# A mask DMA put behind q's low half, twelve weight chunks converted on one engine less, and another order of work

## The chip, the cores and the metric

The kernel runs on one core of one Trainium2 chip. The metric is the device time of one execution in microseconds (us). TensorE is called PE below (its weight loads PEld), VectorE DVE, ScalarE ACT, GpSimd POOL, SyncE SP.

## The reference, cut to what matters

```python
# attention: batch 2, 8 heads, 768 positions, head size 64, 16 cluster centres a head
q_assign = argmax(q_n @ c_n);  k_assign = argmax(k_n @ c_n)
scores = where(q_assign[:, None] == k_assign[None, :], q @ k.T / 8, -1e9)
x = softmax(scores) @ v                        # 1536 tokens x 512
h = x @ w_in                                   # 512 -> 2048
g = where(h >= 1, h, where(h <= -1, 0, (h + 1) ** 2 / 4))
x = g @ w_out                                  # 2048 -> 512
out = ((x @ w1) * (x @ w2)) @ w3 @ w_out2      # 512 -> 1024 -> 1024 -> 512
```

All arithmetic is float32. The weights come to the kernel as float64 words.

## The kernel before

**Work and stages.** Matrix products in float32 precision are made of products of a high and a low half (`hi`, `lo`): x = hi + lo, and three of the four partial products are summed. Attention goes by units: unit u is a pair of heads of one batch (u = 0 to 3 batch 0, 4 to 7 batch 1), each with heads h = 0 and 1. A unit has two groups of 384 query positions and in each of them six tiles s of 128 queries against 768 keys, so 48 tiles a batch (`s` 0 to 47 and 48 to 95). A tile is `s` (PE, scores), `smax` (DVE, L867), `sbias` (POOL, L872), `sexp` (ACT, L880), `spT` (PE, transpose, L897), `sT` (copy to SBUF, ACT or DVE), and six tiles later `pv` (PE, product with v). Batch 0's attention runs beside the preparation of the last two weight matrices (`wp`, L1169: w3 @ w_out2 beforehand); after it come the MLP products of batch 0 beside batch 1's attention, then the MLP of batch 1 alone.

**Halves of q and k.** For head h of a unit, `kh` and `qh` copy the high halves into place, `klo` and `qlo` subtract to get the low halves (POOL or DVE), `k2h`, `q1h` and `qh0` copy a half to the other partitions. Tile kq2 holds q's and k's high halves; its rows 64 to 79 carry, at the time of the product, the cluster mask. For h = 1, `qh` (L678) first writes q's high half into rows 64 to 127 of kq2, `qlo` (L690) reads it there, and `qh0` (L684) puts a copy into rows 0 to 63. The operation `k2` (`kq_fill`, L713) fetches the mask rows by two DMAs on ACT's queue (batch 0), one for each half of the columns. `s` needs `klo`, `qlo`, `k2`, `k2h` and `q1h` of its head.

**Weight chunks.** `chunk` (L1094) loads 128x512 float64 words as pairs of 32-bit words and makes float32 of them: `wl` (DMA on ACT's queue), `wabs` (ACT, L1107: the high word as a float, scaled, so that its bits lie right but for a shift by 3), `wr` (ACT, L1111: the low word scaled by 2^-29, in place, written as an integer), `wc 2` (DVE, L1115: shift left by 3, or the low bits), `wc 3` (DVE, L1121: or the sign). Then `whi` (ACT or DVE) and `wlo` (POOL or DVE) split the chunk, or, for chunks that are kept for later, `wd` writes it to DRAM (SP's queue). Chunks 0 to 39 are converted while batch 0's attention runs, 40 to 71 in the MLP of batch 0.

**The order.** The program's order is written out: ORDER (L38) has two characters for each of 3036 operations; they are a number in base 88 whose half is the operation's place in the sequence of `add` calls, and whose last bit chooses the first or the second engine that the operation may run on. `order` (L126) reads it, and every engine gets its instructions in that order. So a position below is a place in ORDER, and an engine works its own operations off one behind the other. A `needs` entry binds the order to come; the semaphores themselves follow from the order and from what each instruction reads and writes. Forty `idle` operations (L469) are dummy matmuls that stand among the first 60 PE operations.

Of the kernel before, what the change touches and what calls it, by code (L numbers as in the profile page):

```python
# [13 lines left out]
U32 = mybir.dt.uint32  # L14
AF = mybir.ActivationFunctionType
ALU = mybir.AluOpType
# [27 lines left out]
    ",(+m<8<s<6&D<F+w&9%@+y+|,#,*,,,6<:<<&K<J<L<N&I,.+e,8,:,<&N,%<g,0<?<@,2,><V<w<e=*,@,L,B,N,D,F+g,P,R,X,Z,]=:,_"
    "<i<Z;|<0<2<k<]<n,e<p<`<a,T,H,J,V,a+i+l,u,w,y&P<u<y<|=J=#-(&@-*-,+o<B<Q<R=,=.=0,c,|-#=X-4-6=<=>=@,g&B&L=i-.-%"
    "-8=2-:&S+r=y=5=6=B=D+s<q=%=(-0-2=N=L-<-@-B,i-D=P=R&T=U=V->=]>0=Z-F&c=m>@-L-X>#=k,k-N-Z=_=a&Y=o,m,o=d-u-H-P-R"
    "-w=q=s>P=|-]&_,r=f-_-e-g-J-y>%=8=F>2=H>a&k>4-a.(.*.,-T,s-V-c>(&[>o>+>6>8&W>:>D-|=g&e=u=w>-?#&b>B>F%*&^%B>H.4"
    ".#...%.6.8&m&i&v>K>L>T-i-k-m-o?4>e.@.0.B.3>.>=>>>R>V&g.:&s?(-q.L.N>X>Z.<.X.Z>c>g>i>q&o>s>u>N.D.F.P.R.T.H.>?F"
    ">l?%?*>w?,>z>n>~.]._.u.a?V.J.V>]?@-s?.?0.c>_/4/(/*/,&z($/@/B.w?2?B?D&w?i?8.m?6?y(-(&%,/.?H&q&|((%D.y?X.|?J/#"
    "?Z/6/8?:?<?>/:/0/<?L?]?N?_?a/%?k?m?o.e/2.g/>?P/D@2?R?q?s?u%.%0%2%4%F/L/N/P/F@B/H?c/J?|@#%H@T/R%6@4%J@,(.?T?e"  # L50
    "?g/X@e%8%:%<0(%L/Z.i.k.o/T0*@6(*@F/]/_@%@(@*.q.s/V@8@:@=@>?w/a/c@./u/w@0@X@D@i0,0.@w/y/|0406%N/m@V@N@H@J/e/g"
    "@L%P0#00%R%T@Z@g@k@]@mA.@o080:@`0%02@b@@@P@R@y0<0>0@0L0B0D0N0P@|A#0X/i/k/oA@AP@qA:A%A)A*0u0w0y0F@c@s0R0H0T@u"
    "0ZA0A20K0WAcA4/rA6A8A,A<A>0]0_0|ADABAF/s(0(2(4(61#0a0cAsAH0e0g1(1*1,14161&ARAgAJAMATAV1.AeAiAk181:AXA]AZ0m10"
# [1704 lines left out]
```

## Time and profile before

| | us |
|---|---|
| three runs | 718.83, 718.34, 717.74 (median 718.34) |
| the profiled execution, its own time | 718.73 |
| its span, first to last instruction | 717.0 |
| PE busy in the span | 697.8 |
| DVE busy | 617.9 |
| ACT busy | 466.6 |
| POOL busy | 278.0 |

Busy is the time in which an engine had an instruction in work; for PE the ends are modelled. Stretches are given from the span's start. 1.7 us of the profiled execution lie around its span.

### The profile page before, as it was taken

How to read it: one execution, taken by the hardware profiler on the slowest of the kernel's cores; microseconds unless marked ns; L12 is line 12 of the kernel's file. 1: busy time of each engine (PE TensorE's matmuls, PEld its weight loads, DVE VectorE, ACT ScalarE, POOL GpSimd, SP SyncE). 2: the span in 40 equal slices, each digit the busy share in tenths (PEclk: the TensorE clock that was granted, in tenths of full speed). 3: DMA queues.
4: the chain of work that ended last, by engine and by line, in shares of the span. 5: the costliest groups of instructions: out<-in, count | busy, mean ns of one | idle time of the engine just before them, and what ended most of it. 6: DMA issues, size and time to landing. Idle time of an engine off the chain costs nothing.

```text
span 717.0 us, 11999 instructions
## 1 busy us (share of the span) xinstructions
PE 697.8 (97%) x4173; PEld 631.0 (88%) x4173; DVE 617.9 (86%) x1091; ACT 466.6 (65%) x871; POOL 278.0 (39%) x349
## 2 busy tenths in 40 slices
PE   5999999999999999999999999999999999999998
PEld 2866777667798999899999999999999999999997
DVE  6989999989888799988999998669988888999941
ACT  7989999878796976897867565235844434544210
POOL 3333524221354522444363232315842643188500
PEclk9999999999999999999999999999999999999999
DMA  8356786876989988998989996654122121222121
GB/s 316 124 196 216 253 257 199 284 236 212 238 189 187 220 228 198 194 261 216 236 218 234 232 221 161 163 200 135 59 74 75 59 88 30 75 75 59 59 81 67
DMA packets 125645, 122.37 MB, mean 171 GB/s; under 512 B 83792, under 2 KB 92432, under 8 KB 125584
## 3 DMA queue, kind: packets, MB, share of 16 engines
q1 hardware_dynamic: 103024, 62.18, 35.4%
q10 hardware_dynamic: 22560, 59.42, 26.4%
q8 instruction: 33, 0.54, 0.3%
q14 instruction: 28, 0.23, 0.1%
HBM read 75.79 MB, written 22.28 MB: 137 GB/s over the span
## 4 chain that ended last, share of the span: by engine, by line
PE 80%; ACT 7%; DVE 7%; DMA 3%; issue 2%; ACTq 0%; POOL 0%; SPq 0%; DVEq 0%
PE mo L1239 37%; PE sc L1492 8%; PE sc L859 8%; PE sc L1239 6%; PE mo L1492 5%; PE mo L1169 3%; PE av L976 3%; PE av L968 3%; PE av L1492 2%; PE sc L897 2%; DVE nm L867 2%; ACT pt L352 1%; ACT w L1111 1%; PE av L1239 1%; DMA pt<-phl 1%
## 5 line engine op out<-in xcount | busy, mean ns | idle before, releaser
L1239 PE MATMUL mo<-X,whl 128*128 128x384 f32 x924 | 170.4, 338 | 0.0
L1239 PEld LDWEIGHTS mo<-X,whl 128*128 128x128 f32 x924 | 160.7, 188 | 2.8 <-issue 0.9
L1239 PE MATMUL mo<-G,whl 128*128 128x384 f32 x720 | 133.3, 340 | 0.0
L1239 PEld LDWEIGHTS mo<-G,whl 128*128 128x128 f32 x720 | 126.6, 188 | 1.1 <-issue 0.3
L357 POOL TENSOR_TENSOR whl<-wf,whl 128x512 fp32r<-128x512 f32 x61 | 83.0, 1363 | 102.6 <-ACT whl L352 51.8
L867 DVE TENSOR_REDUCE nm<-sc 128x1 f32<-128x768 f32 x96 | 89.9, 950 | 11.2 <-PE sc L859 11.0
L872 POOL TENSOR_SCALAR nm<-nm 128x1 f32<-128x1 f32 x96 | 32.0, 334 | 126.9 <-DVE nm L867 123.3
L352 ACT ACTIVATE whl<-wf 128x512 fp32r<-128x512 f32 x69 | 43.1, 627 | 43.8 <-PE mo L1239 16.1
L859 PE MATMUL sc<-k,q 128*128 128x512 f32 (+1 forms) x192 | 53.7, 361 | 4.2 <-ACT pt L352 2.6
L1111 ACT ACTIVATE w<-w,down 128x512 uint32<-128x512 uint32 x72 | 54.3, 764 | 3.4 <-DVE wf L1121 2.4
L357 DVE TENSOR_TENSOR phl<-sc,phl 128x768 f16<-128x768 f32 x46 | 43.7, 951 | 10.6 <-ACT phl L352 10.1
L1107 ACT ACTIVATE wf<-w 128x512 f32<-128x512 f32 x72 | 48.1, 671 | 5.4 <-DMA wd<-wf 2.1
L1115 DVE SCALAR_TENSOR_TENSOR wf<-wf,w 128x512 uint32<-128x512 uint32 x72 | 49.0, 685 | 1.9 <-ACT wf L1107 1.2
L1121 DVE SCALAR_TENSOR_TENSOR wf<-w,wf 128x512 uint32<-128x512 uint32 x72 | 49.2, 690 | 0.9
L880 ACT ACTIVATE sc<-sc,nm 128x768 f32<-128x768 f32 x46 | 39.8, 866 | 15.2 <-POOL nm L872 15.0
L859 PE MATMUL sc<-kq 80*128 80x512 f32 (+1 forms) x192 | 49.5, 339 | 0.0
L880 ACT ACTIVATE P<-sc,nm 128x768 f32<-128x768 f32 x50 | 44.8, 898 | 7.1 <-POOL nm L872 2.3
L357 DVE TENSOR_TENSOR whl<-wf,whl 128x512 fp32r<-128x512 f32 x51 | 39.7, 779 | 7.3 <-ACT whl L352 7.0
L859 PEld LDWEIGHTS sc<-k,q 128*128 128x128 f32 x192 | 31.5, 189 | 12.7 <-ACT pt L352 5.5
L897 PEld LDWEIGHTS sc<-ident,P 128*128 128x128 f32 x300 | 33.5, 140 | 9.6 <-ACT P L880 5.9
L897 PE MATMUL sc<-ident,P 128*128 128x128 f32 x300 | 39.5, 275 | 2.1 <-ACT P L880 2.0
L1239 PE MATMUL sc<-G,whl 128*128 128x384 f32 x204 | 37.8, 339 | 0.0
(235 smaller groups left out, 1435.1 us busy)
## 6 DMA issues: line engine op xcount, KB each, us to landing
wf<-wd ACTq DMA_DIRECT2D x64, 256.0 KB, 2.8
w<-in_w_out_dram ACTq DMA_DIRECT2D x24, 512.0 KB, 5.1
wd<-wf SPq DMA_DIRECT2D x48, 256.0 KB, 3.5
w<-in_w3T_dram ACTq DMA_DIRECT2D x16, 512.0 KB, 3.9
w<-in_w_in_dram ACTq DMA_DIRECT2D x16, 512.0 KB, 4.7
w<-in_w_dram ACTq DMA_DIRECT2D x16, 512.0 KB, 4.8
wp<-wf SPq DMA_DIRECT2D x16, 256.0 KB, 3.2
wf<-wp ACTq DMA_DIRECT2D x16, 256.0 KB, 2.9
```

The source lines that it names most:

```text
L352: nc.scalar.activation(out=out, in_=in_, func=AF.Copy)
L357: (nc.gpsimd if e == "POOL" else nc.vector).tensor_tensor(out=out, in0=a, in1=b, op=ALU.subtract)
L859: nc.tensor.matmul(ps[:, n], q[0:n_rows, q0:q0 + 128], k[0:n_rows, n], start=first, stop=not first)
L867: nc.vector.tensor_reduce(out=nm, in_=T[("sc", b), s], axis=AX.X, op=ALU.max, negate=True)
L880: nc.scalar.activation(out=new(("P", b), s).rearrange("p n s -> p (n s)") if by_pe(s) else T[("sc", b), s], in_=T[("sc", b), s], func=AF.E ...
L897: nc.tensor.transpose(T[("sc", b), s][:, c], p[:, c], ident)
L1107: nc.scalar.activation(out=T["wf", i], in_=T[w64, i].bitcast(F32)[:, :, 1], func=AF.Abs, scale=float(2.0 ** -112))
L1111: nc.scalar.activation(out=lo, in_=lo, func=AF.Identity, scale=float(2.0 ** -29 - 2.0 ** -41), bias=down)
L1115: nc.vector.scalar_tensor_tensor(out=w, in0=w, scalar=3, in1=T[w64, i][:, :, 0], op0=ALU.logical_shift_left, op1=ALU.bitwise_or)
L1121: nc.vector.scalar_tensor_tensor(out=w, in0=T[w64, i][:, :, 1], scalar=0x80000000, in1=w, op0=ALU.bitwise_and, op1=ALU.bitwise_or)
L1239: nc.tensor.matmul(acc, w[:, a, k4 * 128:(k4 + 1) * 128], rhs(c, k4), start=(first and k4 == 0 and n == 0), stop=(last and k4 == 3 and n = ...
L1492: nc.tensor.matmul(ps, lhs(av, a, k), rhs(bv, c, k), start=k == 0 and n == 0, stop=k == 1 and n == 2,)
```

## The change

Three edits. First, the need of `k2` in batch 0 for h = 1 is `qlo` in place of `qh`. In the old order `k2` stands ahead of `qlo` for units 1 and 2 (positions 220 and 224, 438 and 468), and behind it for units 0 and 3; in the new one it stands behind it for all (25 and 107, 210 and 239, 432 and 447, 567 and 619).

Second, for chunks 1, 3, ... 23, `wr` on ACT is left out. DVE does it: `wc 1` (tensor_scalar, shift left by 3, in place) and `wc 2` (scalar_tensor_tensor, low word shifted right by 29, or the result).

Third, ORDER is another string of the same length. PE's operations of batch 0's attention follow nearly the same sequence. What differs ahead of the last `pv` of batch 0 (position 885 in both), read from the two strings, is where operations run:

| operation | ACT before, after | DVE before, after | POOL before, after |
|---|---|---|---|
| wr | 40, 28 | | |
| wc 1 to 3 | | 80, 92 | |
| klo, qlo | | 12, 7 | 8, 13 |
| kh, qh, qh0, k2h, q1h | 26, 30 | 15, 11 | |
| sT | 42, 41 | 6, 7 | |
| ri (reciprocal rows to SBUF) | 5, 7 | 3, 1 | |
| whi | 6, 8 | 19, 17 | |
| wlo | | 9, 10 | 16, 15 |

`klo` and `qlo` of batch 1 are on POOL 6 times before and 11 times after. At the start `qlo 0 0` and `klo 0 0` go from DVE to POOL; POOL's sequence becomes `qlo 0 0`, `klo 0 1`, `klo 1 0`, `qlo 1 0`, `klo 0 0`, `sbias 0` (before: `klo 0 1`, `klo 1 0`, `qlo 1 0`, `sbias 0`). On ACT `qh 1 0` stands right behind the first mask (`ah 0 k 5 0`); before, a second mask instruction (`am0 k 0`) stood between them. `k2 1 0` goes from position 235 to 86.

```diff
@@ ORDER: all lines
-    "###%#*#,#0#.#(#2$2$V%X%[#4%e%h$.%V%c%q$0$6$8$:#R#>%b$<%m$X$]#D$_$a#8#:%k%_:m$>%y&,:|;0%]%i$c$4$H$J;>#V$@$B$D"
...
+    "###*#,#%#0#(#.#2#4$V%X%Z$.%c$X$0$4$]%e%q%V%i%_%y:m%h%m:|;0;>%];L&,$6$8$:$<$_$a$>$c$e$2$H#P$@$B$J$g$Z$q#H$s$,"
...
@@ k2
-                    else [("qh", u, h)] + [("ah", 0, w, 5, j // 2) for w in "kq"],
+                    else [("qlo" if h else "qh", u, h)] + [("ah", 0, w, 5, j // 2) for w in "kq"],
@@ chunk
+        def shift(e):
+            w = T["wf", i].bitcast(U32)
+            nc.vector.tensor_scalar(out=w, in0=w, scalar1=3, scalar2=None, op0=ALU.logical_shift_left)
+
+        def low(e):
+            w = T["wf", i].bitcast(U32)
+            nc.vector.scalar_tensor_tensor(
+                out=w, in0=T[w64, i][:, :, 0], scalar=29, in1=w, op0=ALU.logical_shift_right, op1=ALU.bitwise_or
+            )
...
-            add(("wr", i), {"ACT": 0.56}, t - 8.5, low_floor, [("wl", i), "c_const"])
-            add(("wc", i, 2), {"DVE": 0.6}, t - 7.8, shift_low, [("wabs", i), ("wr", i)])
+            if i % 2 and i < 24:
+                add(("wc", i, 1), {"DVE": 0.34}, t - 8.2, shift, [("wabs", i)])
+                add(("wc", i, 2), {"DVE": 0.6}, t - 7.8, low, [("wc", i, 1)])
+            else:
+                add(("wr", i), {"ACT": 0.56}, t - 8.5, low_floor, [("wl", i), "c_const"])
+                add(("wc", i, 2), {"DVE": 0.6}, t - 7.8, shift_low, [("wabs", i), ("wr", i)])
```

## Rows read from the trace of the kernel before

**Rows 1.** Windows: PE, PEld, DVE, ACT, POOL busy (count), PEclk, DMA share, GB/s.

```profile
0.00:18.00 18.00, 10.14 (x57) 4.58 (x58) 12.45 (x33) 13.45 (x18) 5.84 (x15) 1.00 0.85 315
18.00:198.00 180.00, 173.56 (x1057) 129.58 (x1056) 167.59 (x266) 157.91 (x273) 58.24 (x85) 1.00 0.70 221
198.00:702.00 504.00, 502.52 (x3000) 485.64 (x2999) 436.30 (x791) 294.76 (x581) 213.04 (x250) 1.00 0.60 150
```

**Rows 2.** Windows within 18 to 198 us, the same columns.

```profile
18.00:72.00 54.00, 51.30 (x334) 39.50 (x333) 49.92 (x84) 49.42 (x86) 18.75 (x28) 1.00 0.54 179
72.00:126.00 54.00, 53.57 (x312) 39.62 (x310) 51.38 (x80) 51.85 (x90) 20.51 (x25) 1.00 0.72 236
126.00:198.00 72.00, 68.69 (x417) 50.45 (x415) 66.29 (x104) 56.63 (x99) 18.97 (x33) 1.00 0.79 241
```

**Rows 3.** Waits, 0 to 198: who, for whom; total us, times, longest.

```profile
PE sc L859 <- ACT pt L352: 2.6, 7, 1.2
ACT sc L880 <- POOL nm L872: 2.6, 2, 1.7
...
ACT wf L1107 <- DMA wd<-wf: 2.1, 1, 2.1
```

**Rows 4.** Groups, 0 to 198 us: count, busy us, mean ns, idle before.

```profile
L352 ACT ACTIVATE pt<-sc 128x768 f32<-128x768 f32 x42 | 32.7, 808 | 4.7 <-PE sc L897 3.8 <-PE sc L859 0.3 <-DVE nm L867 0.2
...
L1111 ACT ACTIVATE w<-w,down 128x512 uint32<-128x512 uint32 x40 | 30.2, 767 | 1.7 <-issue 1.0 <-DVE wf L1121 0.7
L1115 DVE SCALAR_TENSOR_TENSOR wf<-wf,w 128x512 uint32<-128x512 uint32 x40 | 27.1, 685 | 0.7 <-ACT w L1111 0.4 <-ACT wf L1107 0.2
...
L352 ACT ACTIVATE kq<-kq 64x768 fp32r<-64x768 f32 x10 | 8.4, 837 | 0.6 <-DMA kq<-in_qT_dram 0.5
L357 POOL TENSOR_TENSOR k<-kq,k 64x768 fp32r<-64x768 f32 x4 | 8.2, 2047 | 12.1 <-ACT k L352 8.2 <-DVE k L354 3.9
...
L354 DVE COPY pt<-sc 128x768 f32<-128x768 f32 x6 | 5.6, 949 | 0.0
...
L354 DVE CAST kq<-kq 64x768 fp32r<-64x768 f32 x10 | 5.5, 553 | 0.2
...
L357 DVE TENSOR_TENSOR q<-kq,kq 64x768 fp32r<-64x768 f32 x5 | 4.8, 952 | 1.5 <-DMA kq<-mask 0.9 <-ACT kq L352 0.6
...
L354 DVE CAST whl<-wf 128x512 fp32r<-128x512 f32 x11 | 4.6, 420 | 0.2
...
L352 ACT ACTIVATE whl<-wf 128x512 fp32r<-128x512 f32 x7 | 4.3, 629 | 0.0
...
L357 DVE TENSOR_TENSOR whl<-wf,whl 128x512 fp32r<-128x512 f32 x6 | 4.1, 680 | 0.0
...
L352 ACT ACTIVATE rb<-mo 128x384 f32<-128x384 f32 x5 | 2.4, 486 | 0.8 <-PE mo L954 0.7
...
L354 DVE COPY rb<-mo 128x384 f32<-128x384 f32 x3 | 1.6, 549 | 0.0
```

**Rows 5.** Timeline of 5 to 21 us: start, us, what, [idle before <-releaser].

```profile
10.15 0.58 DVE L555 STREAM_TRANSPOSE P<-sc 128x384 f32<-128x384 f32 x1 [1.45 <-PE sc L539]
...
11.35 0.95 DVE L357 TENSOR_TENSOR k<-kq,k 64x768 fp32r<-64x768 f32 x1
...
16.85 0.84 ACT L352 ACTIVATE kq<-kq 64x768 fp32r<-64x768 f32 x1
...
17.77 1.82 POOL L357 TENSOR_TENSOR q<-kq,kq 64x768 fp32r<-64x768 f32 x1 [3.19 <-ACT kq L352]
...
20.19 0.62 PE L859 MATMUL sc<-k,q 128*128 128x512 f32 x2 [0.26 <-DVE kq L590]
```

**Rows 6.** Waits of 198 to 717, columns as in rows 3.

```profile
ACT sc L880 <- POOL nm L872: 12.4, 11, 2.8
```

**Rows 7.** Lines 354, 357, weights only: ns minimum/median/maximum, first and last start.

```profile
L354 DVE CAST whl<-wf x43: 385/419/1207, 51.1 to 692.4; 128x512 fp32r<-128x512 f32 x43
...
L357 POOL TENSOR_TENSOR whl<-wf,whl x61: 1264/1295/2082, 43.7 to 701.6; 128x512 fp32r<-128x512 f32 x61
```

More of the change, by code (lines that the diff above doesn't have):

```diff
@@ L44 @@
[L44 to L53, printed above, removed]
@@ new lines @@
+    "+B;g&>+D*i*k*o;s+<<T+0+2+L+N+P+X+Z+]<(;u&&<*&/&:<6<,&5<.;x;y&D+F+R+>+_;Z;j;k&<%(<c+H*r*s+T+a+u+J+V<s+c+w+y,4"
+    ",(,*,,,6,8<8<:<F<<<H<J<L<N%%+e&F&I<X+m<?+|,#<@,.,:,0,<&K&8,%=*,2,>,@<V,L,B,D+g=:,N,P,X,Z,]&N<e<g<i<Z<k<]<n,F"
+    ",R;|<`<a<0%><2,u<u<p,_,T,H,J+i,a&@,w+k+o<w<y=J,V=X,y,|,c,e,g<|=#<B<Q<R&P-(-*+r=,=>=<-4-#-6=i&B-,-.=.=0=@=2%@"
+    "=B=D=5-%&M-8-:+s<q=%=(-0-2&c=6-<,i-@-B-D=L=]=y=Z=N=P=_=R=U->>0-X,k-F=a=d=e-L-N,m-P-Z-]&j-H&T-u-w-K=k=V&Z&X>@"
+    "&W=m=o>P>#,o=q-R-_-e=8=F=H-g=s&_.(-a.*=|>2,q-T-V>a-c-y&]-|>D&k,s>%>(>o>4>+>6&S>->8>:>B>F&b>H&n=g=u&o=w&e.4.6"
@@ new lines @@
+    ".#.,...%?#>J>L-m>e-i-k-o.@.0?4.B.3&g&s>.>=>>>R>T.L.N>V.8.:.<.X.Z?(>X%B%*-q>N>c>q>g>Z&u.D.F>s.P.R.T.>>i?F?%?*"
+    ">u?,.]._.H.J.a?V.V.u>w>l?/>n>z&q.c?1>~/(/4>]?@&w(,>_&y&|/@?6?H?i?J(%?Z.w-s?8?X/B/*.y.|/D/,?2?B?D.m($%,/6/8/."
+    ".e()/:%D(.?:?<?>?L?]?_?a/#?m/%/0/<?k?o/2/>?y?N?P?R(*?q?s%.%0%2%4%F/L/N/P/F/H.g?u%H%6%J@2@B/J?c?T?e@#@,?|/X/R"
+    "%L?g%8%:%</Z/]/T@T.i.k.o0(0*0,@%@(@*@4?w@.@0/_.q.s/a/V/c@D/u/w/y%N@F@H@J@L@e0.@6/|@8@:0406@<@w@?A.@X/m00@V/e"
+    "/g@i@N%P%R%T080:@g0#0&02@@@Z@]@_@k@q@m0<0>@a@|@P@y@R@oA:0L0@0N0P0X/i/kA@0B0DA2A#/oA%A)A*0u0w@c@s@u0y0ZAP0R0F"
@@ new lines @@
+    "0T0H0KA0A4Ac0|0]0_0W/rAs/sATA,A<A>0e0a0c0gA6A8AD(01((2ABAR1*1,1.Ag141#1618AFAH(4(6AV0mAXAZAwAJAeAiAM101%120i"
+    "0kAuAkAn0oAo1X1ZA]1@1L(:(91N1BB%B,ANA_(<(>AyA|B#Aa1:1]0r1P(B(M1R(A(N1D1F1<1>1_1e1g(D(FAqB(B*1H1T1J1V1a1d(HFL"
+    "BJBi1i1l0s(J2*2,2.20B/1u1w1y22C.B01|(P(R241m1o1r(T1s(V2#2%BL2(BN26(X28B2B4B6BlB82:2<(ZB>B;C0CLB@2F2H2>2A2B2D"
+    "BBBDBmCk2JB]B_2LBbBc2N2PB=2RBFBPC2CNBRFe2T2VCQB|BTC#C%BIC(BVC@2c2e2X2ZCB2]BX2_CE2gBeBg2i2l2m(]BZBoBqBsCFCmCo"
+    "Bu2a2oD0C*CRCTC,CVBx3%3(D>3*3436CICJFPDL3,CX3/3032C4C6BzC8C:CqCsCuDZCwC=Cz383:C|D33<3>3@D#3B3D3F(_D5CZC^D%(a"
@@ new lines @@
+    "D(G#C_C>3P3R3TDACaDODB2y3H3K3LD63NCcCeD*Di3_DD3V3Y3Z3]G((c(e(gDQD-3mD:2qE.EL3a3c3e3gD.2sDFChD93o3q3i(lDHD]D_"
+    "DK3sD<DR3v3w2u2xDk3k(m3yDVE0EkDTDX(o(j(t(u(q3|40424#4>4@444649DeDh2|DmDa4%EO4BFiF04:4<4D4GE2D|EP4HF>CiDcFNFR"
+    "FT4(DoEnEo4L4N4PE#4Z4]4_E%E(Dq3#GLFgFkFVFm4RE@EB4T4VE*EDE,EFDsE4E6(wDu4J4XF2F4(yDxDyFoE8GuE:EI4a4c4eE<E>4*4,"
+    "EK4.4gG%G*G,(|)#)%G.ER4iETEWE_EaEcF@FB4kGy4mEXGPHDEeEqEh5:5<EsGNGRGTF:GV4oEuEw4qEj4s4uF#5>5@F<5C5D5FFXF6F8FZ"
+    "GwE[Ez4w4yE]F%F(F*E~4|5#G|H#HmF]5,5.F_5%FqFs)()*5(5*HF5H5J5LFHFJI,FDFFF-G0G3HHHJ5NFaFcGY5PGZHL5V5R5T5XHoHq),"
@@ new lines @@
+    ").HsHuHwFyF|ID5Z5]I]5eFu5g5i5_H%Fw)4F/5a5c5k)0H(H*G@GBGDI05mI.)2GFGH5oHNG4G6G8G]G_IFHQGJHRG:GaG<Ia5s5u5w5yGc"
+    "IH6(6*6,GfI2I4Gh5|6#G?IJ)8IL545052Iu565q58GiGkHyH|GmI_I6GoGrGtIc)<H8H:H<H>H,H.H06.60Ie6R6THTHVJDI9H2H4666%Ig"
+    "62INJm);)6)>64HaHcIQ6D6F6VHYH@HfHZ6X6Z6]I:I#I%I(IwHgIy6H6JI|J#JHJFJJHj6a6c6e)@6L6N6_JLISI@IBHkI*6g6iJ%6PH^I<"
+    "I>JqIiJ(J*H`6kIXIZ6o6q6sHBIkJoK4JsJuH6)B6>JN6m)D6uKT6w6y6|K6J87#7%K8K:J:KuJ<J>K<IT)F)H)J)LJQ7(7*JwK>IVIq7N7P"
+    "7RKVKXKZIsJSImJAJzJ|K]K_7,Io7.707TL<68KyJCJ,J.J0J2J5J7JTJVLTJXJZJ^J`)N)P7V7X7ZK@JaJcJeKBJgL@JiJkKwL>6:6<7274"
@@ new lines @@
+    "76K#K%K(787:KaKcLBK*K|LDL#Lu7<7>KDKF7]KHKLKNKPL%K,KJL(LVLX7_7a7c7eK.K1KRL+K2KmKo7k7m7oM47g7iLZ)SKqKsLw7qL]Ly"
+    "6@)T7s7u7wMTL,L4L6L8M8KeL.L0L:LHM6LaKgKiL2LKL|7y7|LF)V)X)ZKk8#8%8(M#MmM(7@M:7BMX8.7H80828486MV8*M<LP8,Ld88LL"
+    "LNM+LR8<8>8@M@LmMCL_)]7D8X8Z8]Lo8BN46BM>MZ8J8_Lq)_7G)h8:LeLgMqLiM]MaMcLsLk8EMD8FM,7J)iM%8HMoM.MF8aM0)aN8MsMu"
+    "My8cNL8g8i8kM|8mN6Nm)kM37LMLN:N<Me8u)cN@NBMiMkMIMKNP)m8L8p8qMNNN8w8yNq8|8eM_8sMw)eMQMhMSN>NRNTNYNZ8RN,N.NHN0"
+    "O,N2)oNo9#N#OLNJ)qNDNsNu)s9%9(O0N%N(9*9,NyNG8N8P989:N]N_O.ONO2N~O4NaOPOe9.90O9O;OR9<9>92OT94NeNgO6NV9@9BP,OX"
@@ new lines @@
+    "OZ96N+O(O*ODOF9FO#OgOHPDOiNcOJ9H9c9e9J9LOkNjOmNkNw9gO&OaOdOqOs9N9P9DOV9RO<O>P0P.P2P49iO@9TP8O]O_Pe9k9q9sOuOw"
+    "OC9m9oOoP;P#9V:%9X9uPHPFPJ8TPL9w9y:(:*9|P%:#Q#P@PN9]PPPS:4PTP)Pi9ZPgP+:,:.8VP6PkPmOzPq:0:2Q(Pt:6Q%PB:8Q*Q,::"
+    ":<O~:>:@P<P>P]:PQDPVQ0Q.PoP_:RPX:B:D:F:H:K:LQN:T:VPu:_:Y:Z:NPyPw:]P|QFQIQ2Q4Q<Q>Q6P[QaQJPaQPQkR#Q@Q9Q:PdQS9_"
+    "9aR.:aQCQLQcQfQTQW:c:fQmQo:gS0QZQ^:iR@QiSASCRcR_S2:kQgR%R)QXR1R3RaR]RfS4RhSEQwQzRjQqQtS6S;Q_S$RyRJS]S_SLRqRm"
+    "S8R|RCS=SPQuQ|RERpSSRtS(S&SfShS+SUR,SmSoSiSqToR*SHSuR:R=S?RlR4SyRFRHRMROR7StTqR8SWSaS,SdT(SxT0RuS/SXSlS[T#Rx"
@@ L96 @@
+    "f#gLfXfif&fmf(hehog6fofqgyh+fZgNgJgHg|h.hgh2h0hih#h4h,hHfkfgfsfugVgXh6h8hrgZg_fwg]hsh(gcgfggh<hBgPgahmhDh>i("
+    "i*hLh@gihJhkhNhThPglgmhRhFhVh_hahci2iDhXi,i.i0h|h[h]hui$iNi4i6i8i>iFiQiIiLi:iaicifiJhwhyi<i%ikiniRiZiiigi^i_"
+    "iTiWiXioiAiqitiBiuiwiyi|"
 )
```

64 lines of the change are left out of this document (18 added, 46 removed).

## The prediction

> **What bounds the kernel now.** I read the stretches first, since a share of busy time over the whole span mixes stages. From 198 to 702 us PE is busy 502.52 of 504.00 us [rows 1]: there PE is the bound, and all that a change of order can win visibly is 1.48 us. The first 18 us have PE busy for 10.14 us; most of the rest passes before its first matmuls, while loads land. Between them, from 18 to 198 us, PE is idle for 180.00 - 173.56 = 6.44 us [rows 1], and here the next two engines are nearly full as well: DVE is busy 167.59 us (93%), ACT 157.91 us (88%), POOL only 58.24 us (32%). The granted clock is 1.00 in all these stretches, the higher of its two levels, so no part of the time is owed to it.
>
> The reader should then cut this stage in three [rows 2]. From 72 to 126 us PE (53.57 of 54.00), ACT (51.85) and DVE (51.38) are all full. From 18 to 72 us PE is idle 54.00 - 51.30 = 2.70 us, and from 126 to 198 us 72.00 - 68.69 = 3.31 us. What PE waits for is seen in the waits [rows 3]: ACT's eviction of the transposed scores ended 2.6 us of PE's idle time in 7 pieces; and ACT itself once waited 2.1 us for the landing of a converted chunk's DMA, because `wabs` of a later chunk needs that buffer. So the stage is bound by three engines in a ring, PE to DVE to ACT to PE, with four score banks between them, and not by one of them.
>
> **The change part by part.** The sums go over the operations ahead of batch 0's last `pv`, counted from the table in the section on the change.
>
> ACT loses 12 `wr` of 767 ns, 9.20 us [rows 4]. It gains 4 copies of halves at 837 ns (3.35), 2 copies of reciprocals at 486 (0.97), 2 high halves of weights at 629 (1.26), and loses one eviction at 808 (0.81): -9.20 + 3.35 + 0.97 + 1.26 - 0.81 = **-4.4 us**.
>
> DVE gains 12 shifts. The trace of before has no tensor_scalar of 512 SBUF words. The nearest rows are the cast of 128x512 from SBUF to SBUF, one input, 420 ns, and the shift-or of two inputs over the same words, 685 ns [rows 4]. I take 420, since the shift too has one input in SBUF and the same size, and keep 685 as the other end: 5.04 us, or 8.22. The second DVE instruction, `low`, reads the same two tiles as the shift-or in its place and is taken at the same 685 ns, no cost. Then DVE loses 5 subtractions at 952 (4.76), 4 casts at 553 (2.21), 2 copies at 549 (1.10), 2 casts at 420 (0.84), and gains one eviction at 949 and one low half of weights at 680: 5.04 - 4.76 - 2.21 - 1.10 - 0.84 + 0.95 + 0.68 = **-2.2 us** (+0.9 us with the dear shift).
>
> POOL gains 5 subtractions at 2047 ns and loses one low half of weights at its median of 1295 [rows 4, 7]: +8.9 us on 58.24, which leaves it two thirds idle. Its cost is not in its load but in its queue (a rival, below).
>
> In a ring of engines the stage can shrink by no more than the smaller relief of the two that carry it, if the other end of the ring, PE, has that much idle time to give. DVE's 2.2 us is the smaller and PE's 6.44 is enough. That is the term that I take: **-2.2 us**. Its bounds are 0 (PE is full where the relief falls) and ACT's -4.4 (DVE's work is covered, ACT alone decides).
>
> **The start.** Before, the first score tile starts at 20.19, released by the DVE mask of q; DVE began on the cluster assignment at 10.15 and had a subtraction of 0.95 us in that chain [rows 5]. In the new order 12 DVE operations of some 0.55 us (0.58 for the one in rows 5) lead from 10.15 to that mask, 18 before, so it would be ready near 10.15 + 12 x 0.56 = 16.9. But `klo 0 0`, which the first tile also needs, now stands on POOL behind `qlo 1 0`, and that one behind `qh 1 0` on ACT. If `qlo 1 0` starts as before, at 17.77 for 1.82 us, `klo 0 0` ends near 19.6 + 1.9 = 21.5, so the first tile starts 1.3 us later. If `qh 1 0` comes forward by 2.6 us from its 16.85 (0.95 for the subtraction that no longer stands in the chain, the rest, an estimate, for the mask and the dummy matmuls that stood ahead), the tile starts about 1.3 us earlier. Both ends are kept; I take 0, because by tile 6 the order has the same ACT work ahead as before, and ACT is then the later engine.
>
> **The mask DMAs.** For units 1 and 2 the low half now goes ahead of `k2`. Before, DVE's `qlo` waited for the mask's landing, 0.9 us of idle time [rows 4]; that goes, at most 0.9 us of DVE. In its place the DMA issue on ACT's queue waits for `qlo`, and all of ACT's queue behind it (`wabs 8`, `kh 2 0`, `sexp 9` for unit 1). Between `qh 1 1` and that issue ACT has a copy of a half (837), a reciprocal copy (486) and an eviction (808) to do, 2.1 us, and POOL's subtraction takes 2.05 [rows 4]: nothing is lost if POOL starts at once, up to 2.0 us of ACT if another subtraction is ahead. The tile that needs the mask follows over 50 positions later. Taken at 0. `k2 1 0`, moved to position 86, waits on ACT's queue for the first two masks, which precede it; 0 too. For the SP queue nothing moves past a wait that is new.
>
> **After 198 us** the string differs everywhere, but PE has 1.48 us to win there and, in a stage in which PE is full, DVE (436.30 of 504) and ACT (294.76) have slack. I take 0, with -1.5 and +1.5 as bounds. The tail after the last matmul has the same operations at its end.
>
> Sum against the profiled execution: 718.73 - 2.2 = 716.5. It stands 0.39 above the median 718.34, so against the median: **716.1 us**.
>
> **The Trainium skill speaks against one part.** First the rows: a DVE cast of weights takes 419 ns at the median and 385 at least, but 1207 once; POOL's subtraction of weights 1295 and up to 2082 [rows 7]; within 0 to 198 us the casts average 420 [rows 4], so there hardly any of this is seen. The Trainium skill, SBUF — State Buffer, section "Who interferes with whom", says that DVE and GpSimd share a port pair which one of them holds for a whole instruction: a tensor_scalar in a two-port mode, or a DVE instruction with two SBUF inputs, shuts out a GpSimd instruction that reads SBUF, and the reverse. By that rule the twelve shifts and POOL's extra subtractions would stand in each other's way, and the third rival would come out; the rows of 0 to 198 us do not bear that out, those of later stretches do.
>
> **The rivals.**
> 1. *The relief falls where PE is full.* For: PE, ACT and DVE are all full from 72 to 126 us [rows 2], and part of the idle time after 126 goes back to a DMA's landing [rows 3], which no engine's relief shortens. If the 2.2 us lie evenly over the 180 us, only the first 54 us can use their share, 0.7 us: 718.34 - 0.7 = 717.7, no change.
> 2. *More than forecast.* The start wins its 1.3 us, and the wait for the landing at the chunk's buffer (2.1 us of ACT, its longest piece at PE 1.2 [rows 3]) goes with the order: 716.1 - 1.3 - 1.2 = 713.6.
> 3. *DVE and POOL hold each other up.* A shift that meets POOL loses up to 1207 - 419 = 0.79 us [rows 7]. POOL is then busy for (58.24 + 8.9) / 180 = 37% of the time: 12 x 0.37 x 0.79 = 3.5 us more on DVE, which turns -2.2 into +1.3: 719.6, no change by the measure, though above. Against: no such cast in this stage.
> 4. *POOL's queue becomes the wait: slower.* `sbias`, 1 operation of every tile, stands in POOL's queue, and ten subtractions more (5 in each batch) of about 2.05 us are put there. Already ACT waited for POOL's bias 2 + 11 times, 2.6 + 12.4 us, 1.15 us each [rows 3, 6]. Ten more waits are 11.5 us of ACT; in batch 1 there are only two score banks to cover them. It is slower once more than 2.2 + 1.4 = 3.6 us of these reach PE; with half of them, 5.7 us, the time is 716.1 + 5.7 = 721.8. Against: after 198 us, PE showed 1.48 us of idle time in spite of 11 such waits.
> 5. *The shift runs at the dear price* (685 ns): DVE's relief is +0.9, none: 718.3.
>
> That the change doesn't do what it says is no rival: the instructions are counted from the string itself.
>
> **How the numbers follow.** A difference under about 0.2%, 1.4 us, can't be told from none with this kernel, so faster means under 716.9 and slower over 719.8. Forecast 716.1: 0.40. Rival 1: 0.25. Rival 2: 0.13. Rival 3: 0.06. Rival 4: 0.13. Rival 5: 0.03. Faster: 0.40 + 0.13 = 0.53; same: 0.25 + 0.06 + 0.03 = 0.34; slower: 0.13. The range runs from 713.2, just under rival 2's time, to 720.0, just over rival 3's; it leaves out rival 4 (0.13) and the far sides of these two (some 0.05). The forecast's own range, with the start's 1.3 us and the bounds after 198 us, is 714.5 to 717.6.
>
> **What would show it.** Right: L1111 falls from 40 to 28 ahead of 198 us, a tensor_scalar group of 12 at about 0.42 us appears on DVE, PE's idle time from 18 to 198 us falls from 6.4 to about 4.2 us, and the start of the stage in which PE is full comes some 2 us earlier. The start: the first tile between 18.9 and 21.5 us. Wrong: waits of ACT or PE for POOL's bias that grow by more than 4 us (rival 4); shifts far above 0.42 us (rivals 3 and 5); PE idle from 18 to 198 us unchanged while ACT's and DVE's busy time fell (rival 1); new idle time of PE after 198 us of more than 1.5 us, which would show that the new string was worse in the stage that I take as unmoved.

## The result, and the profile of the changed kernel

The changed kernel takes **726.13 us** (median; 724.20 to 735.48) beside 718.04 for the kernel before in the same comparison: a ratio of 1.0086, interval 1.0056 to 1.0115. It is slower, by 4 to 8 us, where 716.1 and a gain were forecast. (The ratios leave out executions that are over 1.5% above the fastest of their kernel, here the one of 735.48; the medians do not.) The profiled execution took 724.61 us, 5.88 more than the profiled one of before, with a span of 722.9.

The same stretches as in [rows 1] and [rows 2], of after (PE, PEld, DVE, ACT, POOL busy, PEclk, DMA share, GB/s):

```profile
0.00:18.00 18.00, 10.06 (x52) 3.67 (x53) 10.59 (x30) 12.96 (x18) 8.91 (x16) 1.00 0.88 326
18.00:198.00 180.00, 173.42 (x1061) 130.18 (x1060) 168.60 (x270) 154.31 (x265) 59.29 (x86) 1.00 0.69 221
198.00:702.00 504.00, 498.49 (x2968) 480.11 (x2967) 438.42 (x797) 289.86 (x566) 219.83 (x258) 1.00 0.62 148
```

From 18 to 198 us PE is idle 6.58 us, against 6.44 before: nothing is won where I expected the win. From 198 to 702 us it is idle 5.51 us, against 1.48: the loss is in the stage that I took as unmoved. What PE waits for there, in the waits of after from 198 to 702 us:

```profile
PE sc L859 <- DVE phl L357: 4.1, 2, 3.4
```

One of these two waits has 3.4 us. (`phl` is the buffer with the high and the low half of a tile's softmax weights, `pt` what the transposing DMA makes of it.) The chain of work around it (start, us, what), in order of time:

```profile
286.77 0.95 DVE phl L357
...
287.75 11.67 DMA pt<-phl
...
299.44 0.82 ACT phl L352
...
300.29 0.97 DVE phl L357
...
301.30 0.96 PE sc L859 x4
```

VectorE finishes the low half of tile 67's softmax weights, and its transposing DMA lands only 11.67 us after its issue. Batch 1 has two `phl` buffers, so ScalarE can write tile 69's high half only then; it has two score banks, so PE can start tile 71 only when VectorE has made tile 69's low half. PE stands, and then runs slower (windows of after, columns as above):

```profile
298.00:300.00 2.00, 0.00 (x0) 0.00 (x0) 0.03 (x1) 0.65 (x2) 0.00 (x0) 1.00 1.16 352
300.00:302.00 2.00, 0.70 (x4) 0.61 (x4) 1.29 (x2) 1.97 (x5) 0.71 (x1) 1.00 1.05 281
302.00:304.00 2.00, 2.00 (x16) 1.05 (x16) 1.71 (x3) 2.00 (x5) 1.88 (x3) 0.59 1.12 260
304.00:306.00 2.00, 2.00 (x16) 1.16 (x14) 2.00 (x4) 2.00 (x5) 0.23 (x1) 0.55 0.52 128
```

Behind the idle stretch the granted clock is 0.59 and 0.55 of full speed for 4 us, most of that time at the lower of its two levels: 4 x (1 - 0.57) = 1.7 us of matmul lost. With the 3.4 us of standing that is 5.1 of the 5.88 us.

The DMAs issued ahead of it, from the timeline of after (the row at 282.07 holds the transposing DMAs of tiles 65 and 67, at 282 and 287.75):

```profile
277.81 0.92 SPq L513 DMA_DIRECT2D raw<-in_kT_dram  x1
278.50 0.33 ACTq L1101 DMA_DIRECT2D w<-in_w_out_dram  x1
278.78 0.42 SPq L513 DMA_DIRECT2D raw<-in_qT_dram  x1
282.07 9.29 SPq L927 DMA_TRANSPOSE pt<-phl  x2
282.66 0.36 ACTq L1101 DMA_DIRECT2D w<-in_w_out_dram  x1
286.89 0.34 ACTq L1101 DMA_DIRECT2D w<-in_w_out_dram  x1
```

From 277.81 to 282.66 us the new order issues unit 6's raw k and raw q (384 KB each) and two 512-KB weight loads, three of the four right ahead of tile 65's transposing DMA. In the order of before the two raw loads stand apart and earlier (timeline of before):

```profile
265.27 0.40 SPq L513 DMA_DIRECT2D raw<-in_kT_dram  x1
...
273.34 0.90 SPq L513 DMA_DIRECT2D raw<-in_qT_dram  x1
```

The rest of after answers to [rows 4] and [rows 5]. Groups up to 198 us:

```profile
L1111 ACT ACTIVATE w<-w,down 128x512 uint32<-128x512 uint32 x28 | 21.3, 768 | 1.1 <-POOL k L357 0.8 <-ACT whl L352 0.2
...
L354 DVE CAST whl<-wf 128x512 fp32r<-128x512 f32 x11 | 5.5, 500 | 0.1
...
L1121 DVE TENSOR_SCALAR wf<-wf 128x512 uint32<-128x512 uint32 x12 | 5.0, 419 | 0.0
```

Timeline of the start:

```profile
18.57 2.20 POOL L357 TENSOR_TENSOR k<-kq,k 64x768 fp32r<-64x768 f32 x1
...
20.52 0.56 DVE L590 TENSOR_SCALAR kq<-sc 16x384 fp32r<-16x384 f32 x1
...
21.22 0.59 PE L859 MATMUL sc<-k,q 128*128 128x512 f32 x2 [0.25 <-DVE kq L590]
```

### The profile page after: what moved, and what is told of

Read it like the earlier page. It is cut to its first block, busy times and chain, and to the rows that moved or that the text cites. A ratio compares the mean times of both kernels' runs of the same rounds, so it can differ in the third digit from the quotient of the medians.

```text
span 722.9 us, 11976 instructions
## 1 busy us (share of the span) xinstructions
PE 699.4 (97%) x4173; PEld 631.0 (87%) x4173; DVE 620.9 (86%) x1101; ACT 458.6 (63%) x850; POOL 289.3 (40%) x360
## 4 chain that ended last, share of the span: by engine, by line
PE 74%; DVE 10%; DMA 7%; ACT 5%; issue 2%; SPq 1%; ACTq 1%; POOL 0%; DVEq 0%; POOLq 0%
PE mo L1253 32%; PE sc L1506 7%; PE sc L859 7%; PE sc L1253 6%; PE mo L1506 5%; PE av L976 3%; PE mo L1183 3%; DMA pt<-phl 3%; PE av L968 3%; PE sc L897 2%; PE av L1253 2%; PE av L1506 2%; DVE nm L867 2%; DMA kq<-in_kT_dram 1%; DMA kq<-mask 1%
## 5 line engine op out<-in xcount | busy, mean ns | idle before, releaser
L1253 PE MATMUL mo<-X,whl 128*128 128x384 f32 x900 | 164.2, 338 | 0.0
L1253 PEld LDWEIGHTS mo<-X,whl 128*128 128x128 f32 x900 | 156.7, 188 | 2.3 <-issue 1.5
L1253 PE MATMUL mo<-G,whl 128*128 128x384 f32 x672 | 124.3, 339 | 0.0
L1253 PEld LDWEIGHTS mo<-G,whl 128*128 128x128 f32 x672 | 118.1, 188 | 1.2 <-DVE tmp L1278 0.4
L352 ACT ACTIVATE whl<-wf 128x512 fp32r<-128x512 f32 x77 | 48.2, 628 | 45.1 <-PE mo L1253 16.8
L872 POOL TENSOR_SCALAR nm<-nm 128x1 f32<-128x1 f32 x96 | 27.4, 285 | 115.8 <-DVE nm L867 109.1
L1111 ACT ACTIVATE w<-w,down 128x512 uint32<-128x512 uint32 x60 | 45.5, 763 | 6.8 <-DMA w<-in_w_dram 4.8
L357 POOL TENSOR_TENSOR wh<-ws,wh 128x256 fp32r<-128x256 f32 x42 | 32.0, 770 | 26.2 <-ACT wh L352 16.5
L1253 PE MATMUL sc<-G,whl 128*128 128x384 f32 x228 | 42.3, 339 | 0.0
L1115 DVE SCALAR_TENSOR_TENSOR wf<-wf,w 128x512 uint32<-128x512 uint32 x60 | 41.2, 687 | 1.1 <-ACT wf L1107 1.0
```

The costliest lines, as they stand in the source:

```text
L352: nc.scalar.activation(out=out, in_=in_, func=AF.Copy)
L357: (nc.gpsimd if e == "POOL" else nc.vector).tensor_tensor(out=out, in0=a, in1=b, op=ALU.subtract)
L1111: nc.scalar.activation(out=lo, in_=lo, func=AF.Identity, scale=float(2.0 ** -29 - 2.0 ** -41), bias=down)
L1115: nc.vector.scalar_tensor_tensor(out=w, in0=w, scalar=3, in1=T[w64, i][:, :, 0], op0=ALU.logical_shift_left, op1=ALU.bitwise_or)
L1253: nc.tensor.matmul(acc, w[:, a, k4 * 128:(k4 + 1) * 128], rhs(c, k4), start=(first and k4 == 0 and n == 0), stop=(last and k4 == 3 and n = ...
```

## The experiments

Each changes the order string, the edits or both; the diffs show the string decoded, work by work. The names are those of the code: `s` a score tile, `shi`, `slo`, `sT` its halves and its transposing DMA, `sexp` its exponential, `ul` a raw load of k or q, `wl` a weight load. After 858 pieces of work the old and the new order have done the same set (but for the edits' own operations), so that the two can be spliced there (about 185 us).

**Which part of the string.** First theory: the loss is that one place of the late order. Rival: the edits or the early order cost it, through GpSimd's queue.

```
x1: + edits 1 and 2, after's ORDER[:858] + before's ORDER[858:]
x2: no edits,        before's ORDER[:858] + after's ORDER[858:]
```

> Both edits and the new order up to the 858th piece of work (to about 190 us), then the order of before to the end. Theory 1 (the loss is one place of the new late order: s 71 waits 3.4 us at 298 us for the transposed copy of tile 67, and TensorE's clock drops behind it): this kernel has the old late order, so it is at before's time, 716.5 to 719, with no idle stretch of TensorE above 1 us between 270 and 310 us. Theory 2 (the edits or the new early order cost it, through GpSimd's longer queue): it is as slow as after, 723 to 727.

Measured 719.81 us, ratio 1.0003 (0.9983 to 1.0024): no loss, though the median lies 0.8 us above the range that was named, and PE idle for 0.03 us from 270 to 310 us.

> The reverse: neither edit, the order of before up to the 858th piece of work, then the new order. Theory 1: 723 to 727, with the idle stretch of about 3.4 us ahead of s 71 near 298 us and a granted clock of 0.5 to 0.7 for some 4 us behind it. Theory 2: at before's time, 717 to 719.

Measured 729.45 us, ratio 1.0096 (1.0054 to 1.0139), single executions from 721.5 to 738.6: all of the loss, and more scatter than any other kernel here. The one that was profiled was among the fastest (721.54): a transposing DMA takes 10.4 us to land in it, tile 71 waits 0.8 us, and the clock stays 1.00 behind that wait. So the late half of the string carries the loss, with none of the edits in the kernel; the late landing was in this profile, the long stall was not. The others were not profiled, but the mean granted clock of each is on record: 1.000 in the two of 721.5 us, 0.995 to 0.993 in those from 726 to 731 us, 0.985 in the one of 738.6. They have stretches at a lower clock that the fastest has not; where, is not shown.

**The two raw loads.** After, with unit 6's raw loads issued where before's order has them in relation to the transposing DMAs:

```diff
- sT 63 | ... sT 64 | ... sT 66 | ... ul 6 k | ul 6 q | slo 65 | sT 65
+ sT 63 | ul 6 k | ... sT 64 | ... sT 66 | ul 6 q | ... slo 65 | sT 65
```

> After, with one change: the two 384-KB loads of batch 1's unit 6 (raw k and raw q) are issued earlier on SyncE's queue, k behind the transposing DMA of tile 63 and q behind that of tile 66, so that they no longer stand right ahead of tile 65's. Theory 1, if the pile-up of these loads with the weight loads and the transposing DMAs is what makes tile 67 land 11.7 us after its issue: tile 67 lands within 9 us, TensorE's wait ahead of s 71 is under 1 us, and the time falls to 717 to 720. If the loads have no part in it, the wait stays above 2.5 us and the time at 723 to 727.

Measured 720.82 us, ratio 1.0028 (1.0003 to 1.0054): two thirds of the loss are given back by moving two DMA issues. Time to landing of the transposing DMAs issued from 276 to 300 us, of after and then of this kernel:

```profile
DMA to landing us min/median/max: 3.7/9.2/12.1
```

```profile
DMA to landing us min/median/max: 3.7/3.8/6.1
```

PE no longer waits there for over 0.2 us. In this kernel's profile another wait stands at 191 us (waits of PE, 186 to 310 us):

```profile
PE sc L897 <- ACT P L880: 2.7, 1, 2.7
...
PE sc L859 <- DVE phl L357: 0.2, 1, 0.2
```

Behind it the clock is 0.54 and 0.60 from 194 to 198 us, another 1.7 us. That is 4.4 us of this execution (722.95, above its kernel's median).

**Cover on PE.** In before's order the p-v product of unit 5 stands between tiles 70 and 71; in after's behind tile 71.

```diff
- s 70 | ... s 71 | ... pv 5 0 | ro 5 0
+ s 70 | ... pv 5 0 | ro 5 0 | s 71
```

> After, with one change on TensorE's queue alone: the p-v product of unit 5's first half (3.1 us) and its reciprocal transposes go ahead of s 71 instead of behind it, so that TensorE has work while tile 67's transposing DMA is under way, as in before's order. All loads stay where they are in after. Theory 1 with cover as the second half of the cause: tile 67 still lands 9 to 12 us after its issue, TensorE's idle time ahead of s 71 falls from 3.4 to under 0.7 us, no drop of the granted clock there, 718 to 721. If only the late landing counts and the cover does not: idle above 2 us, 723 to 727.

Measured 728.08 us, ratio 1.0127 (1.0069 to 1.0184), not told apart from after's 1.0086: the expectation fell. In the profiled execution (733.5, the slowest of this kernel) a transposing DMA took 18.0 us to land, and PE waited 6.1 us for tile 71 although the product had been done ahead of it. Cover of 3 us does not help against a landing that can be 6 us later still; what the same loads cost here varies with the execution.

**The other side of the pile.** After, with the raw loads left in place and two weight loads issued later:

```diff
- wl 62 | ... ul 6 k | ul 6 q | slo 65 | sT 65 | ... wl 63 | ... sT 67
+ ... ul 6 k | ul 6 q | slo 65 | sT 65 | wl 62 | ... sT 67 | wl 63
```

> After, with one change on ScalarE's queue: the 512-KB weight load 62 is issued behind tile 65's transposing DMA and load 63 behind tile 67's, instead of ahead of each; the raw k and q loads of unit 6 stay right ahead of tile 65's. Theory 3 (the transposing DMAs land late because they share the 16 DMA engines with too many large loads at once, whichever these are): tiles 65 and 67 land within 9 us of their issue, the wait ahead of s 71 is under 1.5 us, 718.5 to 722.5. Theory 4 (only the raw loads count, since they stand in the same queue ahead of tile 65): still over 10 us and 724 to 728.

Measured 722.80 us, ratio 1.0075 (1.0052 to 1.0098). In the profile the transposing DMAs land within 6.2 us and tile 71 doesn't wait, as theory 3 says; but the time lies just above that theory's upper end and the ratio hardly below after's. What the profiled execution (721.51, the fastest of its kernel) loses is at the place of the next but one experiment, 191 us, where PE waits 2.1 us and its clock is 0.67 and 0.50 from 194 to 198 us; from 198 to 702 us PE is idle for 1.33 us, no more than before. Its other executions were not profiled. It speaks for the sum of the loads and not for the raw loads alone, without settling how much.

**Making before stall.** Before, with the raw loads late and tile 71 ahead of the product, then also with weight load 63 earlier:

```diff
- ul 6 k | ... ul 6 q | ... sT 65 | ... wl 63 | ... s 70 | ... pv 5 0 | ... s 71
+ (wl 63, second kernel only) | ... ul 6 k | ul 6 q | sT 65 | ... s 70 | ... s 71 | pv 5 0
```

> Before, made to look like after in this place alone: the loads of raw k and q of unit 6 are moved from 265 and 273 us to right ahead of tile 65's transposing DMA (about 283 us), and s 71 goes ahead of the p-v product of unit 5's first half. Theory 1: tiles 65 and 67 land 10 us or more after their issue, TensorE stands 2 to 4 us ahead of s 71 near 300 us and its clock drops, 722 to 727. If after's loss has another cause: 717 to 719.5.

> Before, with the late raw k and q loads of unit 6 and s 71 ahead of the p-v product as in the kernel that was tried already, and beside that weight load 63 issued about 4 us earlier, so that three large loads stand within some 4 us ahead of and beside tile 65's transposing DMA (after has four within 5 us). Theory 3: tile 65 or 67 lands 9 us or more after its issue, TensorE waits 1.5 us or more ahead of s 71, 721 to 726. If the number of loads beside the transposing DMA has no part in it: 718.5 to 721, as the kernel without the earlier weight load.

Measured 719.98 us, ratio 1.0015 (0.9998 to 1.0033), and 720.27 us, 1.0029 (1.0011 to 1.0047). The transposing DMAs land within 7.4 and 7.7 us, no later than before's own longest (8.3), and PE waits 0.5 us. The first is not clear of none, the second a small loss, and the intervals overlap; neither is after's. Moving the raw loads away ends the stall in after's order, putting them there in before's doesn't make it. The neighbours that before's order puts elsewhere must count too. Which of them was not tried.

**The second wait.** At 191 us after's order issues weight load 43 ahead of tile 48's exponential on ScalarE's queue, and that issue waits until the buffer's product has landed in DRAM.

```diff
- shi 49 | wl 43 | wlo 40 | sexp 48
+ shi 49 | wlo 40 | sexp 48 | wl 43
```

> After, with one change on ScalarE's queue at 190 us: weight load 43, whose issue waits until the product that VectorE wrote into its buffer has landed in DRAM (6.7 to 8.2 us after its issue in the kernels with the new late order, 4.8 to 5.1 in those with the old one), goes behind the exponential of tile 48 instead of ahead of it. Theory 5 (the new late order has two such places, this one and the one ahead of s 71, and each costs its idle stretch and a lower clock behind it in the runs where the DMA is late): TensorE's wait of 1.1 to 2.7 us at 191 us is gone, the place at 298 us stays; 721 to 726, that is 1 to 3 less than after. Theory 1 alone (only the place ahead of s 71): 724 to 728, as after.

Measured 726.65 us, ratio 1.0125 (1.0101 to 1.0149): no gain at all, as theory 1 alone has it. The wait at 191 us is gone from the profile, the one ahead of tile 71 stands there as in after (waits of PE, 186 to 310 us):

```profile
PE sc L859 <- DVE phl L357: 3.4, 2, 3.2
```

**Both places mended** (the diffs of the raw loads and of load 43 together):

> After, with both places mended: load 43 behind the exponential of tile 48, and the raw k and q loads of unit 6 issued behind the transposing DMAs of tiles 63 and 66. Theory 5: no idle stretch of TensorE above 1.2 us between 186 and 310 us, clock 0.999 or 1.0, 717.5 to 720, a ratio of 0.998 to 1.002, as the kernel with the old late order. If the new late order loses in many small places beside: 1.003 or more.

Measured 719.37 us, ratio 1.0018 (1.0000 to 1.0036), beside 1.0028 with the raw loads alone and 1.0125 with load 43 alone. So within after's order the place of the raw loads carries the loss. Load 43's part can't be told from nothing by these times, though in single executions it costs (4.4 us in the profile with the raw loads alone, 2.1 us of waiting and 1.7 us of clock in the one with weight loads 62 and 63 later). From 198 to 702 us PE is idle 1.78 us in it, and ScalarE still waits 20.8 us for GpSimd's bias, as much as after (windows, then waits of ACT from 198 us):

```profile
198.00:702.00 504.00, 502.22 (x2998) 484.51 (x2997) 440.77 (x797) 290.37 (x567) 220.20 (x259) 1.00 0.61 150
```

```profile
ACT sc L880 <- POOL nm L872: 20.8, 16, 5.1
```

**What the edits cost without the search.** Before's order, with both edits; with the first alone, with the second alone:

```diff
  both, first:  - k2 2 1 | ... qlo 2 1          + ... qlo 2 1 | k2 2 1     (unit 1 alike)
  both, second: - wr i | wabs i | wc i 2        + wabs i | wc i 1 (DVE) | wc i 2     (odd i < 24)
```

> The order of before with both edits in it and nothing else moved: in units 1 and 2 the mask DMAs of the second head go behind q's low half, and each odd chunk's floor on ScalarE becomes a shift on VectorE right ahead of its low-bits step. Theory 1 gives the edits next to nothing: 716.5 to 719.5. Theory 2 (the edits cost): above 720. My recorded sum for the early stage with the new order was -2.2; without a string that is fitted to them I expect no gain above 1 us.

> The order of before with the first edit alone: the mask DMAs of the second head of units 1 and 2 stand right behind q's low half in ScalarE's queue; the chunks are converted as in before. Theory 1b (in the old order it is the added wait that costs: ScalarE stands in its queue behind q's low half of unit 2, which VectorE does 9 us later than the mask DMA stood in before): TensorE idle 4 to 5 us near 101 us, granted clock 0.5 behind it, 724 to 728. Theory 2b (the conversion edit does it): no idle stretch of TensorE above 2 us, 717 to 720.

> The order of before with the second edit alone: each odd chunk below 24 has its floor on ScalarE replaced by a shift on VectorE right ahead of its low-bits step; the mask DMAs stand where they stood. Theory 1b: 717 to 719.5, no idle stretch of TensorE above 2 us (12 floors of 767 ns less on ScalarE, 12 shifts of 419 ns more on VectorE, as in after). Theory 2b: 724 to 728.

Measured 727.15 us (1.0100, 1.0063 to 1.0137), 727.53 us (1.0109, 1.0086 to 1.0132) and 722.20 us (1.0040, 1.0021 to 1.0058). The first expectation fell, the second came as theory 1b had it, with a shorter wait (3.7 us), the third time lies between the two ranges that were named. The first edit costs some 8 us in an order that was not made for it. Its timeline:

```profile
49.31 0.62 PE L859 MATMUL sc<-k,q 128*128 128x512 f32 x2 [2.18 <-ACT pt L352]
...
98.56 0.33 ACTq L1101 DMA_DIRECT2D w<-in_w_out_dram  x1
101.86 1.28 ACTq L728 DMA_DIRECT2D kq<-mask  x2
103.18 0.74 ACT L1111 ACTIVATE w<-w,down 128x512 uint32<-128x512 uint32 x1 [4.16 <-issue]
...
104.86 1.35 PE L897 MATMUL sc<-ident,P 128*128 128x128 f32 x6 [3.71 <-ACT P L880]
```

The mask DMA stood at 88.9 us in before; now ScalarE sits at its issue from 99 to 101.86 us, until VectorE's subtraction of 100.87 is done, and everything in its queue with it; PE stands 3.7 us, and from 106 to 108 us its clock is 0.50. The mask DMA of unit 1 does the same at 47 us: PE stands 2.18 us (the first row), and its clock is 0.62 and 0.52 from 50 to 54 us.

With the second edit alone PE has no wait above 1.6 us, and its idle time from 18 to 198 us is 6.3 us, no more than before. The profiled execution (720.04, the fastest of nine) is 1.3 us above before's. From 198 to 702 us PE is idle 1.35 us more in it, and there is one wait near 220 us that before has not, for a transposing DMA (waits of PE, 18 to 260 us):

```profile
PE av L976 <- DMA pt<-phl: 1.6, 1, 1.6
```

What the other eight executions pay is not shown. The kernel with the early half of the new string has the same wait, 1.7 us, in its profile.

**A splice.** Edits and new order up to the 760th piece of work, old order from there, and unit 0's `klo` ahead of unit 1's `qlo` on GpSimd:

```
+ after's ORDER[:760] + before's ORDER[760:], klo 0 0 ahead of qlo 1 0
```

> A version from what the runs show: both edits and the new order up to the 760th piece of work (162 us), then the order of before, and k's low half of unit 0, which GpSimd does in after behind another subtraction just ahead of the first tile, done ahead of that one. From the profiles of before and after, TensorE loses 20.1 us up to 162 us in the new order against 20.8 in the old one, and from there to 198 us 2.3 us in the old order against 3.4 in the new one; the first tile can start up to 1 us earlier than in after. Expected: 716.5 to 719, a ratio of 0.996 to 1.001. If the early stage is set by other things than these stretches: 1.000 to 1.003.

Measured 718.97 us, ratio 1.0017 (1.0003 to 1.0031): the ratio that was expected did not come, and no version here beats before. The first tile hardly starts earlier than in after (21.22), though unit 0's `klo`, the second of the two subtractions in the first row, is done at 14.75 us:

```profile
10.85 3.90 POOL L357 TENSOR_TENSOR k<-kq,k 64x768 fp32r<-64x768 f32 x2 [0.75 <-ACT k L352]
...
21.18 0.58 PE L859 MATMUL sc<-k,q 128*128 128x512 f32 x2 [0.26 <-DVE kq L590]
```

## Why the prediction was wrong, step by step

- **"After 198 us ... I take 0, with -1.5 and +1.5 as bounds": the step that failed.** With the late string alone it measured 1.0096, +6.9 us (3.9 to 10.0). The 1.48 us that PE had left bounds a gain. It says nothing of a loss, and I used it for both. Slack of DVE and ACT was the wrong cover as well: the wait came from the DMA engines, whose column I had not read. In before it stands at (windows, columns as in [rows 1]):

```profile
198.00:270.00 72.00, 71.87 (x447) 68.09 (x446) 60.99 (x97) 57.33 (x109) 31.07 (x39) 1.00 0.93 206
270.00:290.00 20.00, 20.00 (x115) 19.58 (x114) 18.73 (x33) 14.32 (x27) 6.17 (x9) 1.00 0.84 198
290.00:310.00 20.00, 19.98 (x133) 17.93 (x132) 18.53 (x29) 16.83 (x32) 9.63 (x10) 1.00 1.08 224
```

  A DMA share of 0.84 to 1.08, against 0.60 over the whole stage in [rows 1]: from 198 to 310 us every transfer has others beside it, and a new order of issues there moves landings by whole microseconds.
- **"That is the term that I take: -2.2 us": not there.** Edits and early order alone give 1.0003, +0.2 us (-1.2 to +1.7). The terms behind it were partly right: ACT's busy time up to 198 us fell by 4.1 us (forecast 4.4), the floors by 12, the shift costs 419 ns (taken: 420, dear end 685). DVE's fell by 0.85 us instead of 2.2; 0.9 of the difference is in the eleven casts of weights, 500 ns at the mean against 420 in [rows 4]. And DVE's relief lay in the wrong place. It lost 1.86 us ahead of 18 us (12.45 to 10.59), where two of the five subtractions stood that I had counted, and from 18 to 198 us it is 1.01 us busier than before (167.59 to 168.60). By the prediction's own rule of the smaller relief the stage had nothing to win. ACT's relief of 3.6 us from 18 to 198 us left PE's idle time where it was (6.58 us). Whether that is because PE was full where it fell, the reason of rival 1, was not tried by itself.
- **The start** came out inside its bounds, 18.9 to 21.5, at 21.22 us, but by luck. `klo 0 0` ends on POOL at 20.77, behind `qlo 1 0`, as was worked out; the splice has it ready at 14.75 and its first tile starts at 21.18 all the same. What releases the tile in both is DVE's mask of q (L590, 20.52 to 21.08 in after): the mask of the other half of q's columns, which the new order puts ahead of the tile, and not the one that I had put at 16.9 (it ends at 18.51). "I take 0" was off by 1.0 us, of which 0.1 is left at 202 us, where tile 52 starts at 202.39 against 202.28.
- **The mask DMAs at 0**: right for the string that came with them (1.0003), and owed to it. The mechanism named there, ScalarE's queue standing behind `qlo`, is real; without the new order it costs 1.0109. My bound of 2.0 us was for the new order; the same wait in the old one is 4.2 us of ACT and takes PE's clock with it.
- **Rival 4** (POOL's queue) had the right sign of the result and the wrong cause. ACT's waits for POOL's bias grew from 12.4 to 20.4 us after 198 us, past the 4 us that I had named as its mark. With 20.8 us of them the kernel with both places mended is at 1.0018. The mark was a poor one: a wait of an engine with slack proves nothing until it reaches PE.
- **Rival 3** and the rule of the Trainium skill, SBUF — State Buffer, section "Who interferes with whom": the twelve shifts run from 416 to 428 ns, none held up. Two other instructions were. One cast of weights ahead of 198 us took 1269 ns, where the longest there had been 428; it is the size of the 0.9 us above. A comparison of the cluster assignment (L568) took 1.24 us, against 0.56 before. Both began beside a subtraction of POOL and ended 0.3 and 0.4 us behind it (timeline of after):

```profile
10.96 1.81 POOL L357 TENSOR_TENSOR k<-kq,k 64x768 fp32r<-64x768 f32 x1 [0.75 <-ACT k L352]
...
11.95 1.24 DVE L568 TENSOR_TENSOR phl<-P,amx 128x384 bf16<-128x384 f32 x1
...
194.22 1.29 POOL L357 TENSOR_TENSOR whl<-wf,whl 128x512 fp32r<-128x512 f32 x1 [3.68 <-ACT whl L352]
194.53 1.27 DVE L354 CAST whl<-wf 128x512 fp32r<-128x512 f32 x1
```

  In the kernels with the early half of the new string, with the raw loads earlier and with both places mended the same comparison took 1.52, 1.82 and 1.48 us and ended each time 0.41 to 0.43 us behind POOL's subtraction, however early it began. So rival 3's mechanism is there, as the rule has it, at two instructions and not at the shifts, and it is no part of the loss after 198 us.
- My last sign, "new idle time of PE after 198 us of more than 1.5 us", is what came: 5.51 against 1.48.
- **A slip in the sums.** With the bounds after 198 us alone the forecast's own range is 714.6 to 717.6, and with the start's 1.3 us on either side 713.3 to 718.9, not 714.5 to 717.6; 726.13 lies outside all of them.

## What to carry to other kernels

Idle time of the bounding engine limits what a new order can win, not what it can lose: where the whole string of work is replaced, look at every queue in every stage, and give the loss side its own bound. Look at the DMA share by stretches; where it is near 1, large loads that nobody needs yet are a suspect just ahead of a transfer that frees a buffer on the score path; the same loads put there in before's order cost little, so try the move. A wait added to an in-order queue is as dear as the order around it makes it: the first edit cost 8 us in the order that was not made for it, and both edits together nothing with the early order that was.
